# 512-token blocks in the first expert layer of a fused attention and MoE kernel, with attention steps given out once per group

## Chip, core and metric

The kernel runs on one core of one Trainium2 chip. The metric is device time in microseconds (us), the median of several runs; lower is better. Before the change it is 1564.3 us (three runs, 1563.93 to 1564.42).

## What is computed

Cut from the reference, with 8 samples of 576 tokens, 8 heads of 64, pooling by 8:

```python
k_p = k.reshape(B, H, 72, 8, D).mean(axis=3)
v_p = v.reshape(B, H, 72, 8, D).mean(axis=3)
attn = softmax(scale * q @ k_p^T)
x = (attn @ v_p), heads joined             # 4608 x 512
h = max(x @ w1, x @ w2, x @ w3)            # 4608 x 768
x = h @ w_out                              # 4608 x 512
h = x @ w_in ; g = h - tanh(h)             # 4608 x 2048
out = g @ w_out                            # 4608 x 512
```

## The kernel before

Most matrix products are made of three TensorE matmuls on operands that are split into a high and a low part (names ending in H and L). Attention works on tiles of up to 128 query tokens: 40 tiles, five to a sample (four of 128 and one of 64). A tile's steps are `q_split` (L256, L257), `qk` (scores; the first 8 tiles L271 to L273, later ones L279 to L284), `sm_exp` (row maxima on VectorE, eight exponentials on ScalarE, L300, L303), `sm_div` (L311 to L315), `tr_main` and `tr_left` (transposes L331, L342 and their evictions). Tiles are gathered into units; once a unit is complete, four `av` steps (four matmuls each, L352 to L355) write its tokens of x, one step for each group of 128 features, and ScalarE and VectorE evict them (L359, L360). The transposes and `av` share a PSUM tag with two buffers.

The first expert layer, `moe_group` (L513 to L515), works on blocks of `BA` = 384 tokens, 12 blocks. A block has 18 groups (6 feature columns times three weights); a group is 12 matmuls of 128x128 weights on 384 tokens, evicted by ScalarE (first weight, L517) or as a maximum by VectorE (the other two, L519). Four PSUM buffers hold groups. Finished columns go to DRAM (`hs`, L522). The units follow the blocks: 384, 192, 192 and 384 tokens for two samples.

The order of the work is set by the program: `steps` is the list of all attention steps, and `moe_part` hands out parts of it between groups through `attn_to`, so many that `point(x)` is reached by the end; before the change it does so twice in a group, once in its middle (`mid`, after half of its matmuls) and once at its end. The compiler's scheduler moves instructions somewhat from that order, except those under `keep_in_program_order`. The weights come as 64-bit numbers and are converted by `Conv` (one `step` is one 128x512 piece: L88 on ScalarE, L95 to L101 on VectorE, then a split, L122 and L123). The 18 pieces of w1, w2, w3 are converted while attention starts up; the 32 pieces of the second layer's weights while blocks two and later run (`cv.step` in `moe_part`).

Startup: the steps of block 0 run first, with a conversion after each tile's second `sm_exp`; then four groups of block 0 while the attention of block 1 is made, four groups of block 1, and then blocks 0 and 1 by turns (one conversion for every two groups), up to the attention of block 2. From block 2 on each block gives out the attention of later blocks and 4 conversions; it ends in block 9, and blocks 10 and 11 have none. After that come `h @ w_out` (L647 to L649) and the second layer (L705 to L707, L718 to L720), 4104 matmuls of 512 columns, which the change does not touch.

Of the kernel before, what the change touches and what calls it, by code (L numbers as in the profile page):

```python
# [7 lines left out]
F32 = mybir.dt.float32  # L8
# [5 lines left out]
ALU = mybir.AluOpType  # L14
AX = mybir.AxisListType

B, NH, S, D = 8, 8, 576, 64
POOL = 8
SP = S // POOL
NT = B * S  # L20
# [3 lines left out]
NP = NH // 2  # L24
W2 = 2 * SP
KM = 128
KL = W2 - KM
BA = 384
NA = NT // BA
BB = 512  # L30
NB = NT // BB
# [9 lines left out]
TANH_T = 0.6  # L41
QA = (0.28138769604723224, 0.18210311958591932, 0.5012423839837391)
QB = (0.28138769604723224, -0.6558710200885569, 0.1935810566809675)


@with_exitstack
def moe_chain_kernel(ctx, tc, qt, kt, vm, vl, ident, cst, w123, wo1, win, wout, out):
    nc = tc.nc
    V, A, G, T, Q = nc.vector, nc.scalar, nc.gpsimd, nc.tensor, nc.sync
# [84 lines left out]
    at = pool("at", side="right")  # L134
# [16 lines left out]


    units = []
    for b in range(0, B, 2):
        units += [
            (b * S, [(b, 0, 128), (b, 128, 128), (b, 256, 128)]),
            (b * S + 384, [(b, 384, 128), (b, 512, 64)]),
            (b * S + 576, [(b + 1, 0, 128), (b + 1, 128, 64)]),
            (b * S + 768, [(b + 1, 192, 128), (b + 1, 320, 128), (b + 1, 448, 128)]),
        ]  # L160
    tiles = []
    for u, (t0, tl) in enumerate(units):
        off = 0
# [63 lines left out]
    def v_split(b):  # L227
        vs, vx = vsum.pop(b), vxsum.pop(b)
        for i, m in enumerate((m0, m1)):
            A.activation(VH[:, :, 64 * i:64 * i + 64], vs, AF.Copy, scale=m)  # L230
        for i, m in enumerate((e0, e1)):
            A.activation(VX[:, i::2, 64:128], vx, AF.Copy, scale=m[:96])
        for i, m in enumerate((m0, m1)):
            c = slice(64 * i, 64 * i + 64)
            V.scalar_tensor_tensor(out=VL[:, :, c], in0=vs, scalar=m, in1=VH[:, :, c].bitcast(F32),
                                   op0=ALU.mult, op1=ALU.subtract)
        for i, m in enumerate((e0, e1)):
            c = VX[32:64, i::2, 64:128]
            V.scalar_tensor_tensor(out=c, in0=vx[32:64], scalar=m[32:64], in1=c.bitcast(F32),
                                   op0=ALU.mult, op1=ALU.subtract)  # L240

    qraw, qsp, sct, eT = {}, {}, {}, {}

    def q_load(n):
        b, s, cnt = tiles[n][:3]
        t = at.tile([128, NP, 128], F32, tag="qraw", name="qraw", bufs=2)
        Q.dma_start(out=t[:, :, :cnt],
                    in_=qt[b, :, NP * s:NP * (s + cnt)].rearrange("p (c t) -> p c t", c=NP))
        qraw[n] = t

    def q_split(n):
        cnt = tiles[n][2]
        t = qraw.pop(n)[:, :, :cnt]
        h = at.tile([128, NP, 128], F32R, tag="qH", name="qH", bufs=2)
        l = at.tile([128, NP, 128], F32R, tag="qL", name="qL", bufs=2)
        A.copy(h[:, :, :cnt], t)  # L256
        V.tensor_tensor(out=l[:, :, :cnt], in0=t, in1=h[:, :, :cnt].bitcast(F32), op=ALU.subtract)  # L257
        qsp[n] = (h, l)

    scp, nbs = {}, {}  # L260
# [65 lines left out]
    def tr_main(n):  # L326
        b, s, cnt, u, off, _ = tiles[n]
        eH, eL, _ = etile(u)
        ps = ps2.tile([128, NP, 128], F32, tag="tr", name="ps_tr")
        for p in range(NP):  # L330
            T.transpose(ps[:, p, :cnt], sct[n][:cnt, p, :KM], idt[:cnt, :cnt])  # L331
        c = slice(off, off + cnt)
        A.copy(eH[:, :, c], ps[:, :, :cnt])
        V.tensor_tensor(out=eL[:, :, c], in0=ps[:, :, :cnt], in1=eH[:, :, c].bitcast(F32), op=ALU.subtract)

    def tr_left(n):
        b, s, cnt, u, off, _ = tiles[n]
        eX = etile(u)[2]
        lf = lft.pop(n)
        ps = ps2.tile([128, 2, 128], F32, tag="tr", name="ps_tr")  # L340
        for j in range(2):
            T.transpose(ps[:96, j, :cnt], lf[:cnt, j].rearrange("p a b k -> p (a b k)"), idt[:cnt, :cnt])  # L342
        c = slice(off, off + cnt)
        A.copy(eX[:, :, c], ps[:96, :, :cnt])
        V.tensor_tensor(out=eX[64:96, :, c], in0=ps[64:96, :, :cnt], in1=eX[64:96, :, c].bitcast(F32), op=ALU.subtract)

    def av(u, p):
# [11 lines left out]
        A.copy(h, ps[:, :n])  # L359
        V.tensor_tensor(out=l, in0=ps[:, :n], in1=h.bitcast(F32), op=ALU.subtract)  # L360


    steps = []

    def add(fn, *a):
        steps.append((fn, a))

    ntl = len(tiles)
    n_k, n_v = [0], [0]

    def next_k():
        if n_k[0] < B * NP:
            k_load(*divmod(n_k[0], NP))
            n_k[0] += 1
# [23 lines left out]
    def q_step(n):  # L398
        if n < ntl:
            q_split(n)  # L400
        if n + 1 < ntl:
            q_load(n + 1)

    first_tile = {}
    for n, t in enumerate(tiles):
# [3 lines left out]
    for n in range(ntl + 1):  # L409
        last = n == ntl  # L410
        if not last:
            b = tiles[n][0]
            k = n - first_tile[b]
        aux = []
        if not last and b + 1 < B:
            if b == 0:
                if k == 4:
                    aux = [(k_step, 1, p) for p in range(NP)] + [(v_step, 1, i) for i in range(NP + 2)]
            else:
                if k in (2, 3):  # L420
                    aux += [(k_step, b + 1, p) for p in (2 * k - 4, 2 * k - 3)]
                if k in (3, 4):
                    aux += [(v_step, b + 1, i) for i in range(3 * k - 9, 3 * k - 6)]
        if not last:
            add(qk, n, 0)
            add(sm_exp, n, 0)
        if n:
            add(sm_div, n - 1)
        if not last:
            add(qk, n, 1)  # L430
            if aux:
                add(*aux.pop(0))
            add(sm_exp, n, 1)
        if n:
            add(tr_main, n - 1)
            if not last:
                add(q_step, n + 1)
            add(tr_left, n - 1)
        else:
            add(q_step, n + 1)  # L440
        if not last and b and k == 1:
            add(v_split, b)
        avs = [(av, tiles[n - 1][3], p) for p in range(NP)] if n and tiles[n - 1][5] else []
        while avs or aux:
            for l in (avs, aux):
                if l:
                    add(*l.pop(0))
# [12 lines left out]
    def attn_to(i):  # L460
        while pos[0] <= min(i, len(steps) - 1):
            f, a = steps[pos[0]]
            f(*a)
            pos[0] += 1
# [6 lines left out]
    for _ in range(NP - 1):  # L471
        next_k()
    q_load(1)
    Q.dma_start(out=consts, in_=cst)
    cv = Conv(sta, [w123[i] for i in range(18)],
              split_to([tuple(t[i].rearrange("p a b -> p (a b)") for t in (wH, wL)) for i in range(18)], V))
# [14 lines left out]
    for i, (f, a) in enumerate(steps[:block_end[0] + 1]):  # L491
        if f is av and a[1] == 0:
            v_split(0)
        attn_to(i)
        if f is sm_exp and a[1] == 1:
            cv.step()
            for k in (2 * a[0], 2 * a[0] + 1):
                if k < NP + 2:
                    v_step(0, k)
    for _ in range(NP):  # L500
        next_k()

    def moe_group(j, f, m, mid):
        xh, xl = xT[j]
        if m == 0:
            hsb[j, f] = hp.tile([128, BA], F32, tag="h", name="h")
        t = hsb[j, f]
        i = f * 3 + m
        ps = psm.tile([128, 512], F32, tag="mm", name="ps_mm")
        for kc in range(NE):  # L510
            if kc == 2:
                mid()
            T.matmul(ps[:, :BA], wH[i][:, kc], xh[:, kc], start=(kc == 0), stop=False)  # L513
            T.matmul(ps[:, :BA], wH[i][:, kc], xl[:, kc], start=False, stop=False)  # L514
            T.matmul(ps[:, :BA], wL[i][:, kc], xh[:, kc], start=False, stop=(kc == NE - 1))  # L515
        if m == 0:
            A.copy(t, ps[:, :BA])  # L517
        else:
            V.tensor_tensor(out=t, in0=t, in1=ps[:, :BA], op=ALU.max)  # L519
        if m == 2:  # L520
            g, o = divmod(j * BA, HG)
            Q.dma_start(out=hs[g][f][:, o:o + BA], in_=hsb.pop((j, f)))  # L522
# [3 lines left out]
    def moe_part(groups, upto, every=1, conv=lambda k: True):  # L526

        first = pos[0]

        def pace(x):  # L530
            attn_to(first + (upto - first) * x // (2 * len(groups)))

        for k, (j, f, m) in enumerate(groups):
            if every == 1 and conv(k):
                cv.step()
            moe_group(j, f, m, lambda: pace(2 * k + 1))
            if every > 1 and m == 2 and f % 3 < 2:
                cv.step()
            pace(2 * k + 2)

# [3 lines left out]
    def point(x):  # L544

        j = int(x)
        if j >= NA - 1:
# [8 lines left out]
    cv = Conv(sta, srcs, lambda i, w: tc.keep_in_program_order(Q.dma_start(out=wsc[i], in_=w)),  # L556
              tc.keep_in_program_order)
# [173 lines left out]
    for i in range(len(seq) + LAG):  # L731
        if i < len(seq):
            j, c = seq[i]
# [68 lines left out]
```

## Time and profile before

| | |
|---|---|
| median of 3 runs | 1564.3 us |
| time of the profiled execution | 1563.4 us |
| its span, first to last instruction | 1561.5 us |
| PE busy | 1517.3 us, 97% |
| DVE (VectorE) busy | 1165.9 us, 75% |
| ACT (ScalarE) busy | 831.3 us, 53% |
| POOL (GpSimd) busy | 195.4 us, 13% |
| mean granted TensorE clock | 0.995 |

The busy shares are averages over stages with different limits, so the span is read in stages: startup until PE runs without a gap, the blocks with attention between their groups, the last blocks without it, and the two later products. Time outside the span (1.9 us) lies around the program.

### The profile page before, as it was taken

To read this page: it belongs to the slowest core of one execution; us is meant where nothing else is said; L and a number is where in the kernel's file an instruction comes from. 1 tells how busy PE (TensorE), PEld (TensorE's weight loads), DVE (VectorE), ACT (ScalarE), POOL (GpSimd) and SP (SyncE) were. 2 spreads that over 40 slices of the span, in tenths; PEclk is the share of its full clock that TensorE was granted. 3 is DMA by queue.
4 is the path that set the end of the run, shared out by engine and by line. 5 is a ranking of instruction groups with operands and counts; after the bars stand their busy time and mean duration, and the time that the engine had idled before them with its cause. 6 is when DMAs were issued, how large, how long until landed. Compare 5 with 4: busy or idle time off the path is not lost.

```text
span 1561.5 us, 21533 instructions
## 1 busy us (share of the span) xinstructions
PE 1517.3 (97%) x7544; PEld 1337.2 (86%) x7544; DVE 1165.9 (75%) x2086; ACT 831.3 (53%) x2077; POOL 195.4 (13%) x223
## 2 busy tenths in 40 slices
PE   4799999999999999999999999999999999999999
PEld 3699999999999899888888888888888888888887
DVE  8994877777787861443398888888888888888886
ACT  6753655545555630543365555555555555555554
POOL 4510210202010020740001001010101001010000
PEclk9889999999999999999999999999999999999999
DMA  7552445444343330865400001010100000010000
GB/s 239 188 190 64 144 134 167 139 148 154 124 138 102 108 106 31 287 224 164 153 1 27 27 4 52 1 55 1 33 23 27 27 27 28 1 55 1 28 1 27
DMA packets 71213, 134.65 MB, mean 86 GB/s; under 512 B 11840, under 2 KB 21184, under 8 KB 71104
## 3 DMA queue, kind: packets, MB, share of 16 engines
q1 hardware_dynamic: 71104, 133.27, 26.0%
q8 instruction: 59, 0.97, 0.3%
q14 instruction: 50, 0.41, 0.1%
HBM read 91.82 MB, written 41.42 MB: 85 GB/s over the span
## 4 chain that ended last, share of the span: by engine, by line
PE 89%; DVE 6%; ACT 2%; DMA 1%; issue 1%; POOL 0%; SPq 0%; ACTq 0%; DVEq 0%; POOLq 0%
PE ps_mm L513 9%; PE ps_mm L705 8%; PE ps_acc L720 8%; PE ps_mm L706 8%; PE ps_mm L707 8%; PE ps_acc L719 8%; PE ps_acc L718 8%; PE ps_mm L514 8%; PE ps_mm L515 8%; PE ps_acc L648 2%; PE ps_acc L649 2%; PE ps_acc L647 2%; PE ps_mm L648 1%; PE ps_mm L649 1%; PE ps_mm L647 1%; PE ps_sc L279 1%
## 5 line engine op out<-in xcount | busy, mean ns | idle before, releaser
L513 PE MATMUL ps_mm<-xH,wH 128*128 128x384 f32 x864 | 301.4, 349 | 0.0
L514 PE MATMUL ps_mm<-xL,wH 128*128 128x384 f32 x864 | 291.9, 338 | 0.0
L515 PE MATMUL ps_mm<-xH,wL 128*128 128x384 f32 x864 | 291.2, 337 | 0.0
L693 ACT CAST gH<-w 128x512 fp32r<-128x512 f32 x144 | 89.4, 621 | 301.4 <-DVE w L692 301.4
L705 PE MATMUL ps_mm<-ioH,ctH 128*128 128x512 f32 x576 | 224.2, 389 | 0.8 <-ACT ioH L604 0.8
L706 PE MATMUL ps_mm<-ioL,ctH 128*128 128x512 f32 x576 | 224.1, 389 | 0.0
L707 PE MATMUL ps_mm<-ioH,ctL 128*128 128x512 f32 x576 | 224.1, 389 | 0.0
L718 PE MATMUL ps_acc<-ctH,gH 128*128 128x512 f32 x576 | 224.1, 389 | 0.0
L719 PE MATMUL ps_acc<-ctL,gH 128*128 128x512 f32 x576 | 224.1, 389 | 0.0
L720 PE MATMUL ps_acc<-ctH,gL 128*128 128x512 f32 x576 | 224.1, 389 | 0.0
L694 DVE TENSOR_TENSOR gL<-w,gH 128x512 fp32r<-128x512 f32 x144 | 104.1, 723 | 92.1 <-ACT gH L693 87.2
L513 PEld LDWEIGHTS ps_mm<-xH,wH 128*128 128x128 f32 x864 | 163.8, 190 | 1.1 <-DVE h L519 0.2
L514 PEld LDWEIGHTS ps_mm<-xL,wH 128*128 128x128 f32 x864 | 163.8, 190 | 0.0
L515 PEld LDWEIGHTS ps_mm<-xH,wL 128*128 128x128 f32 x864 | 163.1, 189 | 0.0
L519 DVE TENSOR_TENSOR h<-h,ps_mm 128x384 f32<-128x384 f32 x144 | 79.3, 551 | 90.4 <-PE ps_mm L515 82.2
L605 POOL TENSOR_TENSOR ioL<-ioL,ioH 128x512 fp32r<-128x512 f32 x32 | 49.3, 1556 | 728.5 <-ACT ioH L604 728.5
L705 PEld LDWEIGHTS ps_mm<-ioH,ctH 128*128 128x128 f32 x576 | 108.1, 188 | 23.8 <-ACT ioH L604 1.2
L720 PEld LDWEIGHTS ps_acc<-ctH,gL 128*128 128x128 f32 x576 | 108.2, 188 | 22.4
L719 PEld LDWEIGHTS ps_acc<-ctL,gH 128*128 128x128 f32 x576 | 108.1, 188 | 22.5
L706 PEld LDWEIGHTS ps_mm<-ioL,ctH 128*128 128x128 f32 x576 | 108.1, 188 | 22.4
L718 PEld LDWEIGHTS ps_acc<-ctH,gH 128*128 128x128 f32 x576 | 108.1, 188 | 22.4
L707 PEld LDWEIGHTS ps_mm<-ioH,ctL 128*128 128x128 f32 x576 | 108.0, 188 | 22.4
(106 smaller groups left out, 2840.6 us busy)
## 6 DMA issues: line engine op xcount, KB each, us to landing
hs<-h SPq DMA_DIRECT2D x72, 192.0 KB, 1.9
ioL<-hs SPq DMA_DIRECT2D x54, 256.0 KB, 2.9
kraw<-kt SPq DMA_DIRECT2D x32, 288.0 KB, 3.5
raw<-w SPq DMA_DIRECT2D x18, 512.0 KB, 3.7
xs<-ob SPq DMA_DIRECT2D x36, 256.0 KB, 2.1
ioL<-xs SPq DMA_DIRECT2D x36, 256.0 KB, 2.8
out<-ob SPq DMA_DIRECT2D x36, 256.0 KB, 2.2
qraw<-qt SPq DMA_DIRECT2D x32, 256.0 KB, 3.4
```

Source lines behind the costliest of these rows:

```text
L513: T.matmul(ps[:, :BA], wH[i][:, kc], xh[:, kc], start=(kc == 0), stop=False)
L514: T.matmul(ps[:, :BA], wH[i][:, kc], xl[:, kc], start=False, stop=False)
L515: T.matmul(ps[:, :BA], wL[i][:, kc], xh[:, kc], start=False, stop=(kc == NE - 1))
L519: V.tensor_tensor(out=t, in0=t, in1=ps[:, :BA], op=ALU.max)
L693: A.copy(gH, w)
L694: V.tensor_tensor(out=gL, in0=w, in1=gH.bitcast(F32), op=ALU.subtract)
L705: T.matmul(ps, wh[:, kc], xh, start=(kc == 0), stop=False)
L706: T.matmul(ps, wh[:, kc], xl2, start=False, stop=False)
L707: T.matmul(ps, wl_[:, kc], xh, start=False, stop=(kc == NE - 1))
L718: T.matmul(acc, gH[:, r], oh, start=(c == 0), stop=False)
L719: T.matmul(acc, gH[:, r], ol, start=False, stop=False)
L720: T.matmul(acc, gL[:, r], oh, start=False, stop=(c == NC2 - 1))
```

## The change

`BA` becomes 512: 9 blocks, and a group's 12 matmuls take 512 tokens. Units are now the pieces into which the block borders cut each sample (`pieces`): 512+64, 448+128, 384+192, 320+256 and the same mirrored, 16 units and 40 tiles as before. Three raw query tiles are buffered and loaded two ahead. The transposes of a tile become one step `tr`. In the startup the conversions come after all attention steps of block 0 rather than between them, and the K loads of the next sample before its last tile. In `moe_part`, groups of block 2 and later give out no attention in their middle, and six conversions a block rather than four. The query split of the tiles in block 2 (the third) is pinned to program order.

```diff
-BA = 384
+BA = 512
+def pieces(b):
+
+    at = [0] + [x - b * S for x in range(0, NT, BA) if b * S < x < b * S + S] + [S]
+    return list(zip(at, at[1:]))
...
-    for b in range(0, B, 2):
-        units += [
-            (b * S, [(b, 0, 128), (b, 128, 128), (b, 256, 128)]),
-            (b * S + 384, [(b, 384, 128), (b, 512, 64)]),
-            (b * S + 576, [(b + 1, 0, 128), (b + 1, 128, 64)]),
-            (b * S + 768, [(b + 1, 192, 128), (b + 1, 320, 128), (b + 1, 448, 128)]),
-        ]
+    for b in range(B):
+        for i, (s, e) in enumerate(pieces(b)):
+            units.append((b * S + s, [(b, t, min(128, e - t)) for t in range(s, e, 128)]))
...
-        t = at.tile([128, NP, 128], F32, tag="qraw", name="qraw", bufs=2)
+        t = at.tile([128, NP, 128], F32, tag="qraw", name="qraw", bufs=3)
...
-        V.tensor_tensor(out=l[:, :, :cnt], in0=t, in1=h[:, :, :cnt].bitcast(F32), op=ALU.subtract)
+        r = V.tensor_tensor(out=l[:, :, :cnt], in0=t, in1=h[:, :, :cnt].bitcast(F32), op=ALU.subtract)
+        if units[tiles[n][3]][0] // BA == 2:
+            tc.keep_in_program_order(r)
...
-            add(tr_main, n - 1)
+            add(tr, n - 1)
             if not last:
                 add(q_step, n + 1)
-            add(tr_left, n - 1)
...
+        if f is qk and a == (3, 0):
+            for _ in range(NP):
+                next_k()
         attn_to(i)
         if f is sm_exp and a[1] == 1:
-            cv.step()
...
-    for _ in range(NP):
-        next_k()
+    for _ in range(4):
+        cv.step()
...
-            moe_group(j, f, m, lambda: pace(2 * k + 1))
-            if every > 1 and m == 2 and f % 3 < 2:
+            moe_group(j, f, m, (lambda: pace(2 * k + 1)) if j < 2 else lambda: None)
+            if every > 1 and m == 2:
                 cv.step()
```

How the instructions move, at three places. First VectorE at the start, after the row maxima of the first tile (`nb`). Before:

```order
L300 TENSOR_REDUCE nb<-ps_sc 128x4 x2
L95 TENSOR_SCALAR ma<-ma 128x512
L97 TENSOR_SCALAR ma<-ma 128x512
L99 SCALAR_TENSOR_TENSOR ma<-raw,ma 128x512
L101 SCALAR_TENSOR_TENSOR ma<-raw,ma 128x512
L311 TENSOR_SCALAR su<-su 128x8
L312 RECIPROCAL su<-su 128x8
L313 TENSOR_TENSOR sc<-sc,su 128x576
```

and with the change (L101, L103 and L105 are now the conversion's lines, L259 the query split, L315 to L317 the division):

```order
L304 TENSOR_REDUCE nb<-ps_sc 128x4 x2
L259 TENSOR_TENSOR qL<-qraw,qH 128x512
L315 TENSOR_SCALAR su<-su 128x8
L316 RECIPROCAL su<-su 128x8
L317 TENSOR_TENSOR sc<-sc,su 128x576
L304 TENSOR_REDUCE nb<-ps_sc 128x4
L101 TENSOR_SCALAR ma<-ma 128x512 x2
```

The four conversion instructions that stood between the first tile's maxima and its division are gone from there. Counted over VectorE's list up to the last piece of x of block 1, there are 2 conversions fewer, 2 tiles more and one half of a sample's K sums more than before.

Second, PE where a tile of a later block is transposed (`sc` main part, `lf` leftover). Before:

```order
L515 MATMUL ps_mm<-xH,wL_154 128x384
L331 MATMUL ps_tr<-idt,sc 128x128 x4
L513 MATMUL ps_mm<-xH,wH_137 128x384
L514 MATMUL ps_mm<-xL,wH_137 128x384
L515 MATMUL ps_mm<-xH,wL_155 128x384
L513 MATMUL ps_mm<-xH,wH_137 128x384
L514 MATMUL ps_mm<-xL,wH_137 128x384
L515 MATMUL ps_mm<-xH,wL_155 128x384
L342 MATMUL ps_tr<-idt,lf 96x128 x2
```

and with the change, in the last block that has attention:

```order
L525 MATMUL ps_mm<-xH,wL_166 128x512
L335 MATMUL ps_tr<-idt,sc 128x128 x4
L346 MATMUL ps_tr<-idt,lf 96x128 x2
L523 MATMUL ps_mm<-xH,wH_148 128x512
L524 MATMUL ps_mm<-xL,wH_148 128x512
```

The main and leftover transposes now follow each other directly, and more expert matmuls stand in one piece. Over the whole list PE goes from expert matmuls to attention matmuls 125 times, 189 times before.

Third, PE between the second and the third `av` of a unit, which share PSUM buffers with the first. Before, in block 3:

```order
L355 MATMUL ps_av<-eL,VH 128x192
L513 MATMUL ps_mm<-xH,wH_134 128x384
L514 MATMUL ps_mm<-xL,wH_134 128x384
L515 MATMUL ps_mm<-xH,wL_152 128x384
L513 MATMUL ps_mm<-xH,wH_134 128x384
L514 MATMUL ps_mm<-xL,wH_134 128x384
L515 MATMUL ps_mm<-xH,wL_152 128x384
L352 MATMUL ps_av<-eH,VH 128x192
```

and with the change, in block 5, at a unit of 128 tokens:

```order
L359 MATMUL ps_av<-eL,VH 128x128
L523 MATMUL ps_mm<-xH,wH_143 128x512
L356 MATMUL ps_av<-eH,VH 128x128
L357 MATMUL ps_av<-eH,VL 128x128
L358 MATMUL ps_av<-eX,VX 128x128
L359 MATMUL ps_av<-eL,VH 128x128
L524 MATMUL ps_mm<-xL,wH_143 128x512
```

Six expert matmuls stood there, and now one; at most other places there are twelve now.

## Rows read from the trace of the kernel before

**Rows 1.** The page: span, and busy time, share and instructions of each engine.
```profile
span 1561.5 us, 21533 instructions
PE 1517.3 (97%) x7544; PEld 1337.2 (86%) x7544; DVE 1165.9 (75%) x2086; ACT 831.3 (53%) x2077; POOL 195.4 (13%) x223
```
**Rows 2.** Busy time of each engine by stretches of the span, with clock and DMA.
```profile
core 0: us, PE busy (x) PEld busy (x) DVE busy (x) ACT busy (x) POOL busy (x), PEclk, DMA share, GB/s
0.00:8.00 8.00, 0.46 (x1) 0.29 (x1) 2.33 (x5) 2.83 (x6) 3.64 (x9) 1.00 0.77 241
8.00:83.60 75.60, 50.03 (x238) 42.57 (x238) 71.35 (x147) 52.47 (x210) 38.73 (x60) 0.91 0.63 209
83.60:160.00 76.40, 76.40 (x443) 76.16 (x443) 52.99 (x114) 34.22 (x107) 0.33 (x1) 0.98 0.37 118
160.00:560.00 400.00, 393.59 (x2382) 382.33 (x2381) 304.98 (x693) 231.18 (x869) 52.37 (x87) 1.00 0.43 139
560.00:626.10 66.10, 66.10 (x382) 65.88 (x381) 22.60 (x36) 8.88 (x18) 4.66 (x3) 1.00 0.12 42
```
**Rows 3.** PE's timeline (start, us, engine, line): expert matmuls, 384 and 512 columns.
```profile
599.76 0.33 PE L514 MATMUL ps_mm<-xL,wH 128*128 128x384 f32 x1
...
625.76 0.33 PE L514 MATMUL ps_mm<-xL,wH 128*128 128x384 f32 x1
...
1199.12 0.39 PE L718 MATMUL ps_acc<-ctH,gH 128*128 128x512 f32 x1
...
1203.88 0.39 PE L718 MATMUL ps_acc<-ctH,gH 128*128 128x512 f32 x1
```
**Rows 4.** PE's timeline: two neighbours of an `av` of 192 tokens.
```profile
524.37 0.28 PE L354 MATMUL ps_av<-eX,VX 96*128 96x192 f32 x1
524.48 0.27 PE L355 MATMUL ps_av<-eL,VH 128*128 128x192 f32 x1
```
**Rows 5.** PE's timeline: going over from expert matmuls to attention and back.
```profile
226.77 0.29 PE L279 MATMUL ps_sc<-kbd,qH 128*64 128x288 f32 x1
...
227.17 0.39 PE L513 MATMUL ps_mm<-xH,wH 128*128 128x384 f32 x1
227.39 0.34 PE L514 MATMUL ps_mm<-xL,wH 128*128 128x384 f32 x1
...
228.28 0.60 PE L331 MATMUL ps_tr<-idt,sc 128*128 128x128 f32 x4
228.64 0.42 PE L513 MATMUL ps_mm<-xH,wH 128*128 128x384 f32 x1
228.90 0.33 PE L514 MATMUL ps_mm<-xL,wH 128*128 128x384 f32 x1
```
**Rows 6.** VectorE busy (x) on tiles `ma`, `sc`, `ps_tr`, `qL`, `xL`, `ksum`, in this order.
```profile
0.00:626.10 626.10, 144.50 (x242) 0.99 0.42 136
0.00:626.10 626.10, 94.35 (x232) 0.99 0.42 136
0.00:626.10 626.10, 40.86 (x80) 0.99 0.42 136
0.00:626.10 626.10, 27.03 (x40) 0.99 0.42 136
0.00:626.10 626.10, 29.03 (x64) 0.99 0.42 136
0.00:626.10 626.10, 32.64 (x54) 0.99 0.42 136
```
**Rows 7.** PE's waits from 160 to 560 us: us in total, times, longest.
```profile
PE ps_av L352 <- DVE xL L360: 2.6, 5, 0.8
PE ps_sc L279 <- DVE sc L284: 1.2, 2, 0.9
```
**Rows 8.** ScalarE's timeline: first and last exponential of the first tile.
```profile
12.93 0.32 ACT L303 ACTIVATE sc<-ps_sc,nb 128x72 f32<-128x72 f32 x1 [0.99 <-DVE nb L300]
...
15.02 0.35 ACT L303 ACTIVATE sc<-ps_sc,nb 128x72 f32<-128x72 f32 x1
```

More of the change, by code (lines that the diff above doesn't have):

```diff
@@ L360, in av, with tr @@
         V.tensor_tensor(out=l, in0=ps[:, :n], in1=h.bitcast(F32), op=ALU.subtract)
+    def tr(n):
+        tr_main(n)
+        tr_left(n)
     steps = []
@@ L400, in q_step @@
             q_split(n)
-        if n + 1 < ntl:
-            q_load(n + 1)
+        if n + 2 < ntl:
+            q_load(n + 2)
     first_tile = {}
@@ L473, in moe_chain_kernel @@
     q_load(1)
+    q_load(2)
     Q.dma_start(out=consts, in_=cst)
@@ L769 @@
     qp = q.reshape(B, NP, 128 // D, S, D).transpose(0, 2, 4, 1, 3).reshape(B, 128, NP, S)
-    cuts = {0: (0, 128, 256, 384, 512, 576), 1: (0, 128, 192, 320, 448, 576)}
+    cuts = [[t for s, e in pieces(b) for t in range(s, e, 128)] + [S] for b in range(B)]
     qt = np.stack([
-        np.concatenate([qp[b, :, :, s:e].reshape(128, NP * (e - s)) for s, e in zip(cuts[b % 2], cuts[b % 2][1:])], axis=1)
+        np.concatenate([qp[b, :, :, s:e].reshape(128, NP * (e - s)) for s, e in zip(cuts[b], cuts[b][1:])], axis=1)
         for b in range(B)
```

## Prediction, made before the result was known

> **What bounds the kernel.** The page comes first: PE is busy for 97% of the span [rows 1], so the time is PE's work plus the 44.2 us in which PE stands still. The second view, the busy time by stretches, says where. From the start to 83.6 us PE is idle for 7.5 and 25.6 us; from 83.6 to 160 us it has no gap; from 160 to 560 us it loses 6.4 us; up to 626.1 us nothing [rows 2]. What is left, 4.7 us, lies behind 626.1 us, which the change does not touch. In the stretch from 8 to 83.6 us VectorE is busy for 71.35 of 75.6 us [rows 2]: it makes x for blocks 0 and 1 and converts weights, so VectorE bounds the start. After that PE does. A change of block size therefore has three places to act: the price of PE's work, the VectorE work ahead of the moment from which PE runs without a gap (for short, the filling point), and the waits afterwards.
>
> The third view, PE's timeline, gives the price of an expert matmul. Between the two rows of 384 columns lie 150 matmuls and 26.00 us, between the two of 512 columns 21 and 4.76 us [rows 3]: 173.3 and 226.7 ns. The reader is to see that the pitch, not the 0.33 or 0.39 us of a row, is the cost, since matmuls overlap. At the granted clock of 1.00 [rows 2], that is the 2.4 GHz level, 384 and 512 columns take 160.0 and 213.3 ns; 13 ns are left over in each, whatever its width.
>
> **The change, part by part.** The sum is made against the profiled execution, 1563.4 us (span 1561.5 and 1.9 around it); the median of the runs is 0.9 higher.
>
> *Fewer, wider expert matmuls.* 12 x 18 x 12 = 2592 at 173.3 ns are 449.2 us; 9 x 18 x 12 = 1944 at 226.7 ns are 440.7 us: **-8.5 us**, all of it on PE. The evictions get fewer and wider and the bytes to DRAM stay the same; with VectorE at 76% and the DMA share at 0.43 between 160 and 560 us [rows 2] both stay beside PE's work. Were that cover gone, the eviction would be late for one of four PSUM buffers, which is the first rival.
>
> Against this speaks a rule of the Trainium skill ("TensorE: Matmul & The Clock Gate", Back-to-back issue gap): a warm matmul takes its columns at 2.4 GHz and only 2.5 ns more. By it the term would be 2592 x 162.5 - 1944 x 215.8 ns, or -1.7 us; the rows have 13 ns and decide.
>
> *The `av` matmuls.* There are 256 before and after. Before, 128 have 384 columns and 128 have 192, the latter at 0.11 us [rows 4]: 22.2 + 14.1 = 36.3 us. After, 32 each have 512, 448, 384, 320 and 256 columns, at columns / 2.4 GHz + 13 ns 0.227, 0.200, 0.173, 0.147 and 0.120 us, and 96 have 192, 128 or 64. The trace shows no `av` below 192 columns. The price is at most the 0.11 us of the nearest row, and at least what the line gives (0.04 and 0.07 us for 64 and 128). I take 0.11, because the 192-column row already lies above its line (0.093): 27.7 + 10.6 = 38.3 us, **+2.0 us**, with the other end at -1.5 us.
>
> *Fewer changes of work on PE.* Behind four score matmuls the next expert matmul takes 0.22 us to its successor, behind transposes 0.26 us [rows 5], where 0.173 is normal: 0.05 and 0.09 us for each return. The order has 64 returns fewer. 27 of them are those between a tile's main and leftover transposes: 27 x 0.09 + 37 x 0.05 = **-4.3 us**. The ends are 0 (if 512 columns make the return dearer, which no row excludes) and 64 x 0.09 = -5.8 us.
>
> *The start.* Up to the last x of block 1, VectorE's list has two tiles more. A tile costs it (94.35 + 40.86 + 27.03 + 29.03) / 40 = 4.8 us [rows 6], so +9.6 us; half a sample's K sums, 32.64 / 16 = +2.0 us; and two conversions fewer at 5 x 144.50 / 242 = 3.0 us [rows 6], -6.0 us. That is +5.6; the row sums, reciprocals and wider evictions that these rows leave out make it about +7 us, by which the filling point moves. But PE has done more when it gets there: 51 matmuls of 512 for 48 of 384 (+3.2), four more sets of scores at 0.40 us (+1.6) and two tiles' transposes at 0.36 us for the main part [rows 5] and about 0.1 for the rest (+0.9), and `av` of 512, 448 and 64 for 384, 192 and 192 (+2.3): +8.0 us. So the idle time changes by **-1 us**. The clock averages 0.91 there [rows 2] and should again. The ends: -5 us, if the 4.2 us that VectorE still lost after 8 us go too, and +10 us by the first rival. The queue of loads is no bound: two raw weight pieces fewer are due, against two query tiles, and the DMA share is 0.63 [rows 2]. The postponed conversions are the next to be late: between the filling point and the 18th there are about 12 x 3.0 us of them, ten maxima and three tiles on VectorE, some 55 us with the maxima at 0.5 us or a little more each, against 14 groups of 2.72 and three tiles on PE. A tile there costs PE (542.5 - 2544 x 0.1733 - 6.4) / 32 = 3.0 us [rows 2, 3], so 47 us. The lag of 8 us is just what three groups in PSUM allow.
>
> *The waits afterwards.* A third `av` waits for the first to be evicted: five waits, 2.6 us [rows 7], where one `av` (0.44 us) and six expert matmuls (1.04 us) stood between. So 2.0 us are needed. With the change two places have only an `av` between, one an `av` and one expert matmul (0.67 us): 1.55 + 1.55 + 1.35 = 4.4 us. Two have an `av` of 320 or 384 tokens and three expert matmuls (about 1.3 us): together 1.4 us. Score buffers, which cost 1.2 us [rows 7], have three expert matmuls between at two places rather than six: about 2 us. The rest, 6.4 - 2.6 - 1.2 = 2.6 us, I keep. That is 10.4 for 6.4, **+4 us**. The ends are -4 us (elsewhere twelve matmuls, 2.72 us, now stand between steps) and +12 us, the second rival. Giving out steps once per group is this term; it issues nothing new. The pinned splits and the third query buffer add no instruction.
>
> *The sum:* -8.5 + 2.0 - 4.3 - 1 + 4 = -7.8 us, so 1555.6 us for a profiled execution and 1556.5 us as a median.
>
> **The rivals.**
> 1. *VectorE runs dry in the start, and the kernel is slower.* The conversions filled VectorE while ScalarE made a tile's exponentials, which take 2.4 us (12.93 to 15.37) [rows 8]. In the new list only two of four come before the first x. If all four tiles of block 0 wait that long, the filling point comes 4 x 2.4 = 9.8 us later; and the lag of 8 us then passes the cover in PSUM for some 4 us more. 1556.5 + 13.8 = 1570 us. For it: VectorE has little else there. Against it: two conversions and the query splits remain, tile follows tile with two buffers each, and VectorE's need to convert only falls. It decides from about 8 us of extra VectorE waits before the first expert matmul.
> 2. *Denser attention eats the gain.* 26 tiles now lie in five blocks, 30 in eight before: 9.4 us of expert work a tile rather than 10.0, and six conversions a block. If each short distance drags the next step along, the waits grow by 12 instead of 4 us: 1564.5 us. For it: VectorE's share was 76% already. Against it: from 160 to 560 us PE lost only 1.6%.
> 3. *The gain is larger.* The wider spacing takes waits away (-3 instead of +4) and the start loses VectorE's gaps (-4 instead of -1): 1546.5 us.
> 4. *The 13 ns are not a matmul's own.* If they grew with the columns, the first term would be nothing: 1565 us. Both pitches [rows 3] speak against it. The skill's 2.5 ns would come to nearly this.
>
> **How the numbers follow.** Forecast 0.47, with its own range 1551 to 1562 us; rival 1 0.13, rival 2 0.20, rival 3 0.17, rival 4 0.03. A measurement of this kernel can tell about 0.2%, 3.1 us, from no change, so faster is below 1561.2 and slower above 1567.4. Faster: 0.40 of the forecast, all of rival 3 and 0.03 of rival 2, 0.60. Same: 0.07 + 0.14 + 0.03 of rival 4, 0.24. Slower: rival 1 and 0.03 of rival 2, 0.16. The range 1545 to 1567 us leaves out rival 1 and the last third of rival 3, 0.19 together.
>
> **What the changed profile would show.** Expert matmuls 0.227 us apart; fewer busy us of LDWEIGHTS; PE without gaps from about 90 us on, with some 33 us idle before; about 10 us of waits up to the last attention step, most at the third `av`; the end of the first layer about 8 us sooner than 626.1. Wrong would be a pitch of 512 columns above 0.23 us among attention work, VectorE with more than 12 us idle between 8 us and the filling point, or PE idle in blocks 2 to 6 by more than 15 us.

## The result and the profile after

The change takes 1551.03 us in the median of three runs (1550.85 to 1551.72) against 1564.3 us: a ratio of 0.9917, 95% interval 0.9904 to 0.9931. The forecast was 1556.5 us, so the direction held and the gain came out larger, 13.3 instead of 7.8 us. The time lies at the lower edge of the forecast's own range, 1551 to 1562 us. The profiled execution took 1550.85 us, its span 1548.8 us.

The page's first lines of the change, beside [rows 1]:

```profile
span 1548.8 us, 20108 instructions
PE 1508.3 (97%) x6896; PEld 1250.4 (81%) x6896; DVE 1154.0 (75%) x2050; ACT 823.5 (53%) x2059; POOL 195.5 (13%) x223
```

Weight loads are busy for 87 us less (648 matmuls fewer), PE for 9 us less. Where the gain lies is seen in the busy time by stretches of the change, to be held against [rows 2]:

```profile
core 0: us, PE busy (x) PEld busy (x) DVE busy (x) ACT busy (x) POOL busy (x), PEclk, DMA share, GB/s
0.00:8.00 8.00, 0.46 (x1) 0.29 (x1) 2.50 (x5) 2.99 (x7) 3.65 (x9) 1.00 0.75 245
8.00:83.60 75.60, 53.66 (x244) 44.48 (x244) 71.01 (x153) 57.38 (x235) 35.50 (x60) 0.90 0.68 214
83.60:160.00 76.40, 76.16 (x353) 63.46 (x354) 62.84 (x131) 40.80 (x137) 12.43 (x18) 0.96 0.47 148
160.00:560.00 400.00, 393.88 (x1962) 327.89 (x1961) 297.73 (x654) 217.63 (x805) 48.35 (x72) 1.00 0.42 135
```

Up to 83.6 us PE is busy for 3.6 us more; from 160 to 560 us it loses 6.1 us where it lost 6.4. The first layer ends at 613.5 instead of 626.1 us, 12.6 us sooner, and what follows is as long as before. PE's timeline of the change gives its returns to expert matmuls, behind transposes (at 229.72 us) and behind scores (at 302.73 us), and the new pitch (104 matmuls lie between the last two rows):

```profile
229.58 0.38 PE L346 MATMUL ps_tr<-idt,lf 128*96 128x128 f32 x2
229.72 0.47 PE L524 MATMUL ps_mm<-xL,wH 128*128 128x512 f32 x1
230.03 0.39 PE L525 MATMUL ps_mm<-xH,wL 128*128 128x512 f32 x1
...
302.66 0.23 PE L285 MATMUL ps_sc<-kbd,qL 128*128 128x144 f32 x1
302.73 0.44 PE L523 MATMUL ps_mm<-xH,wH 128*128 128x512 f32 x1
303.01 0.40 PE L524 MATMUL ps_mm<-xL,wH 128*128 128x512 f32 x1
...
589.66 0.39 PE L523 MATMUL ps_mm<-xH,wH 128*128 128x512 f32 x1
...
613.23 0.39 PE L525 MATMUL ps_mm<-xH,wL 128*128 128x512 f32 x1
```

That is 23.57 us / 104 = 226.6 ns, as in [rows 3], and a return costs 0.28 - 0.227 = 0.05 us behind scores and 0.31 - 0.227 = 0.08 us behind transposes, 0.05 and 0.09 us with 384 columns [rows 5]. PE's waits from 160 to 560 us, beside [rows 7], and the three of them that fall on the third `av`:

```profile
PE ps_av L356 <- DVE xL L364: 3.3, 3, 1.7
PE ps_tr L335 <- DVE sc L317: 1.5, 1, 1.5
PE ps_av L356 <- DVE eL L338: 0.6, 1, 0.6
PE ps_sc L283 <- DVE sc L288: 0.6, 1, 0.6
```
```profile
212.84 0.36 PE L356 MATMUL ps_av<-eH,VH 128*128 128x192 f32 x1 [1.69 <-DVE xL L364]
...
364.50 0.36 PE L356 MATMUL ps_av<-eH,VH 128*128 128x192 f32 x1 [0.92 <-DVE xL L364]
...
425.14 0.33 PE L356 MATMUL ps_av<-eH,VH 128*128 128x128 f32 x1 [0.65 <-DVE xL L364]
```

These are the three places named beforehand; no other third `av` waits for an eviction, and scores wait once, for 0.6 us.

**A balance.** Up to the start of the second layer, time is PE's idle time, the time lost at the lower clock, and the rest, which is PE's work at full clock. I add the loss over stretches of 4 us as busy time times (1 - granted clock); that overstates it where little of PE's work slows, so the last column is good to some 4 us. The rows are of the profiled execution of each kernel, in us, which can lie off the median: e1's took 1561.4 us, the fastest of its eleven and 4 us under their median; e3's, e5's, e8's and e9's lie 2 to 3 us off. Run names are explained below.

```
kernel                      median  2nd layer  idle   idle     lower  work
                                    from       0-160  160-560  clock
before                      1564.3  626.1      33.1   6.4       6.8   579.8
the change                  1551.0  613.5      29.7   6.1       7.7   569.9
e1 conversions between      1565.4  623.9      36.9   6.3      10.7   570.0
e2 steps given out twice    1553.8  615.4      30.3   8.1       6.9   570.1
e3 transposes in two steps  1558.8  623.6      33.1   5.9      16.4   568.2
e4 384 columns, all else    1564.2  626.1      29.7   6.8      15.7   573.9
e5 512 columns alone        1563.9  623.8      39.7   4.9       6.0   573.2
e6 384, conversions behind  1559.7  622.2      28.2   6.9      10.4   576.7
e7 no pin                   1551.8  615.2      28.6   6.1      10.6   569.9
e8 low parts on GpSimd      1560.8  621.9      35.1   5.6      14.2   567.0
e9 three pieces first       1561.9  626.2      36.7   6.5      15.6   567.4
e10 five pieces first       1557.3  619.7      32.2   6.0      15.7   565.8
e11 512, conversions behind 1557.4  618.8      31.4   4.9      12.7   569.8
e12 three, own queue        1557.5  621.5      31.9   8.1      11.0   570.5
```

So the change does 9.9 us less work (-10.8 was forecast for the first three terms), stands still for 3.7 us less, and loses 1.0 us more at the lower clock.

### The profile page after: what moved, and what is told of

Its sections match the earlier page's. It is cut to its first block, busy times and chain, and to the rows that moved or that the text cites. A ratio compares the mean times of both kernels' runs of the same rounds, so it can differ in the third digit from the quotient of the medians.

```text
span 1548.8 us, 20108 instructions
## 1 busy us (share of the span) xinstructions
PE 1508.3 (97%) x6896; PEld 1250.4 (81%) x6896; DVE 1154.0 (75%) x2050; ACT 823.5 (53%) x2059; POOL 195.5 (13%) x223
## 4 chain that ended last, share of the span: by engine, by line
PE 89%; DVE 8%; ACT 1%; issue 1%; DMA 0%; ACTq 0%; DVEq 0%; SPq 0%
PE ps_mm L715 8%; PE ps_mm L717 8%; PE ps_acc L730 8%; PE ps_acc L728 8%; PE ps_acc L729 8%; PE ps_mm L716 8%; PE ps_mm L523 8%; PE ps_mm L524 8%; PE ps_mm L525 8%; PE ps_acc L659 2%; PE ps_acc L658 2%; PE ps_acc L657 2%; PE ps_mm L659 1%; PE ps_mm L658 1%; PE ps_mm L657 1%; PE ps_sc L283 1%
## 5 line engine op out<-in xcount | busy, mean ns | idle before, releaser
L523 PE MATMUL ps_mm<-xH,wH 128*128 128x512 f32 x648 | 260.0, 402 | 0.0
L524 PE MATMUL ps_mm<-xL,wH 128*128 128x512 f32 x648 | 254.2, 392 | 0.0
L525 PE MATMUL ps_mm<-xH,wL 128*128 128x512 f32 x648 | 253.8, 392 | 0.0
L529 DVE TENSOR_TENSOR h<-h,ps_mm 128x512 f32<-128x512 f32 x108 | 73.9, 685 | 104.2 <-PE ps_mm L525 102.9
L525 PEld LDWEIGHTS ps_mm<-xH,wL 128*128 128x128 f32 x648 | 121.9, 188 | 25.9
L523 PEld LDWEIGHTS ps_mm<-xH,wH 128*128 128x128 f32 x648 | 122.6, 189 | 22.7
L524 PEld LDWEIGHTS ps_mm<-xL,wH 128*128 128x128 f32 x648 | 122.4, 189 | 22.5 <-DVE xL L364 0.3
```

## Experiments

The first four ran together (the kernel before had 1563.85 us there), then e5 to e8 (1564.42), e9 to e11 (1564.23) and e12 (1563.78). Each ratio is to the kernel before of its own group. The change's three runs had their own (1564.3); a difference from the change is one of medians.

**e1: conversions between the first tiles again.**

```diff
         if f is sm_exp and a[1] == 1:
+            if a[0] < 4:
+                cv.step()
             ...
-    for _ in range(4):
-        cv.step()
```

> The changed kernel, but the first four conversions stand between the tiles of block 0 again. Theory S (the start got shorter because conversions no longer sit ahead of the attention in VectorE's list): PE's idle time before it fills grows by 3 to 4 us, the time is 1554 to 1555 us. Theory F (the start got shorter because PE holds more work when it fills: wider matmuls, two more tiles done): the time stays within 1 us of the changed kernel, 1550 to 1552 us.

1565.36 us, ratio 1.0006 (0.9997 to 1.0014): the whole gain is gone, far more than the 3 to 4 us of the larger expectation, though the work is the same 570 us. Two things are lost in its trace, whose execution is 10.5 us slower than the change's; the other 4 us of the median are in no trace. First, PE is idle for 4.4 us more up to 100 us, and the last x of block 1 comes 4.0 us later (below, e9). Second, PE stands still again at 137 us, long after it had run without gaps, and then runs at the lower clock. PE's timeline of e1, and its windows around:

```profile
139.65 0.33 PE L285 MATMUL ps_sc<-kbd,qL 128*128 128x144 f32 x1 [2.87 <-DVE qL L259]
```
```profile
136.00:140.00 4.00, 1.13 (x7) 0.73 (x6) 3.97 (x8) 1.04 (x3) 2.00 (x2) 1.00 0.41 131
140.00:144.00 4.00, 4.00 (x13) 3.14 (x13) 3.87 (x8) 1.33 (x4) 0.00 (x0) 0.57 0.52 142
```

**e2: steps given out twice per group in all blocks.**

```diff
-            moe_group(j, f, m, (lambda: pace(2 * k + 1)) if j < 2 else lambda: None)
+            moe_group(j, f, m, lambda: pace(2 * k + 1))
```

> The changed kernel, but groups of all blocks give out attention steps in their middle as well. By its order there are 25 more returns of PE from attention to expert matmuls, and none of the five short distances between the avs of one unit. Theory G (giving out once saves returns): 25 x 0.05 to 0.09 = +1.3 to +2.3 us against waits of 3.3 us less, 1549 to 1551 us. Rival (once or twice changes nothing that PE waits for): 1550.5 to 1551.5 us with the waits still there.

1553.81 us, ratio 0.9933 (0.9921 to 0.9945): 2.8 us of the gain, though this interval overlaps the change's (0.9904 to 0.9931), and slower than both expectations. The waits of a third `av` shrink from 3.3 to 0.7 us, but waits for scores (3.6 us) and for the transposed low parts (3.1 us) take their place, 8.1 instead of 6.1 us in all.

**e3: the two transposes apart again.**

```diff
-            add(tr, n - 1)
+            add(tr_main, n - 1)
             if not last:
                 add(q_step, n + 1)
+            add(tr_left, n - 1)
```

> The changed kernel, but a tile's main and leftover transposes are apart again, with the query split between them. 19 more returns of PE and two more short distances between avs. If a return costs 0.05 to 0.09 us: +1 to +1.7 us, and up to 2 us of waits: 1552 to 1555 us. If a return costs nothing: 1551 to 1552 us.

1558.76 us, ratio 0.9965 (0.9953 to 0.9976), 7.7 us slower than the change and slower than both expectations. By the balance the work is no larger, although it has 19 returns more; the loss is 3.4 us of idle time in the first 160 us and about 9 us at the lower clock.

**e4: everything but the width.**

```diff
-BA = 512
+BA = 384
-            if every > 1 and m == 2:
+            if every > 1 and m == 2 and f % 3 < 2:
```

> The changed kernel with blocks of 384 tokens (12 blocks, units of 384 and 192, four conversions a block), every other edit kept. Theory W (the width is worth 8.5 us on the expert matmuls, less 2 us on the avs): 1551 + 6.5 = 1557.5 us, PE's pitch 0.173 us. If the start's gain also needs the width (theory F above): 1560 to 1562 us. If the gain came from the order of the rest and not from the width: below 1555 us.

1564.21 us, ratio 0.9999 (0.9991 to 1.0008), outside all three expectations. The other edits alone give no time: the work falls by 6 us and idle time by 3 us, and the lower clock takes 9 us more. Block 0 is three tiles here, so the conversions behind it come earlier, and PE has no expert matmul for a while. The window from 60 to 80 us of e4, first all of PE's work, then that on the `ps_mm` tiles alone:

```profile
60.00:80.00 20.00, 14.15 (x58) 11.42 (x58) 19.36 (x44) 14.77 (x61) 9.46 (x13) 0.50 0.52 164
```
```profile
60.00:80.00 20.00, 0.00 (x0) 0.00 (x0) 0.00 (x0) 0.00 (x0) 0.50 0.52 164
```

None of the 58 matmuls is an expert's (15 are in the kernel before, 25 in the change), and the clock is at its lower level, 1.2 GHz, for all of the stretch; in the same window it is 0.84 and 0.81 there.

**e5: the width alone.** The edits of e1, e2, e3 and e7 together, and two query buffers. The earlier K loads stay, here and in e11.

> The change's wide blocks with nearly all the rest undone: conversions between the first tiles, two splits for the two tables of transposes, steps given out twice a group, no pin, two query buffers. Theory B (a balance: up to the second layer PE needs 570 us of work at full clock with 512 columns and 580 with 384, and what differs beside that is PE's idle time and the time lost at the lower clock): work 572 to 575 us (47 returns more than the change), idle 40 to 46, clock 7 to 14, so a second layer that begins at 621 to 633 us and 1557 to 1571 us in all, near 1565, as without the width. Theory W (the width is a gain in itself): 1553 to 1558. Theory A (the losses of undoing the edits one by one add up, 14 + 3 + 8 us): 1573 to 1579.

1563.85 us, ratio 0.9998 (0.9989 to 1.0006), near the 1565 that the balance gave: work 573, idle 44.6, clock 6.0 us. The width saves its work and the start gives it back. Theory W falls, and so does the sum of single losses: those of e1, e2 and e3 are partly the same loss.

**e6: the kernel before, conversions behind block 0's attention.**

```diff
         if f is sm_exp and a[1] == 1:
-            cv.step()
             ...
+    for _ in range(4):
+        cv.step()
```

> The kernel before, with four conversions behind block 0's attention instead of one behind each of its tiles. If the place of the conversions is a gain in itself (theory S, the 10 us that the change lost without it): 1551 to 1558. If it needs 512 columns, because with 384 block 0 is three tiles and PE then runs out of expert matmuls while VectorE converts (theory F): 1561 to 1568, with idle time up to 100 us within 3 us of before.

1559.65 us, ratio 0.9970 (0.9959 to 0.9982): between the two expectations. The place of the conversions is worth 4.8 us by itself with 384 columns (4.4 us less idle time, 3.6 us more at the lower clock, 3.1 us less work in the balance, which is within its error).

**e7: no pin.** The pin of the query splits in block three taken out.

> The change without the pinned query splits of block three. The pin only sets VectorE's order in one block. Theory P0 (nothing): 1549 to 1553, with the second layer from 612.5 to 615 us. Theory P (the pin holds a query split back from being taken early or late, so that scores wait): 1553 to 1557, with more idle time of PE between 200 and 300 us.

1551.75 us, ratio 0.9918 (0.9905 to 0.9932): the pin is worth nothing that can be measured.

**e8: low parts of the weights on GpSimd.**

```diff
-              split_to([... for i in range(18)], V))
+              split_to([... for i in range(18)], G))
```

> The change with the low halves of the first 18 weight pieces (18 subtractions of 0.706 us on VectorE) made on GpSimd, where such a subtraction takes 1.8 us. Theory V (VectorE's list sets the start): eight of them lie before PE runs without a gap, 5.6 us; PE is idle for 2 to 5 us less up to 100 us and the kernel takes 1545 to 1549. Theory X (a GpSimd operation behind reductions that wait for loads comes late, or both engines slow each other on SBUF): expert matmuls wait for a wL, 1552 to 1560.

1560.84 us, ratio 0.9976 (0.9967 to 0.9986), 10 us slower than the change: the time of theory X, but not its waits, since no expert matmul waits for a wL. A subtraction took 1.26 to 1.60 us on GpSimd. Nine low parts are now done before block 1's x, which comes at 97.8 us, instead of six and 92.5: VectorE had run the rest of those conversions ahead of it. And some of VectorE's other instructions got longer. The same group on VectorE between 8 and 96 us, the change first, then e8:

```profile
L315 DVE TENSOR_SCALAR su<-su 128x8 f32<-128x8 f32 x8 | 2.1, 258 | 1.7 <-ACT sc L307 1.7
```
```profile
L315 DVE TENSOR_SCALAR su<-su 128x8 f32<-128x8 f32 x8 | 3.4, 422 | 1.7 <-ACT sc L307 1.6
```

**e9 and e10: three or five weight pieces first.** The change makes four pieces behind block 0's attention and then runs four groups of each of blocks 0 and 1 before it interleaves them. For three:

```diff
-    for _ in range(4):
+    for _ in range(3):
         cv.step()
...
-    moe_part(gr(0)[:4], point(2), conv=lambda k: k == 0)
-    moe_part(gr(1)[:4], point(2.2))
-    moe_part([g for p in zip(gr(0)[4:], gr(1)[4:]) for g in p], ...)
+    moe_part(gr(0)[:3], point(2), conv=lambda k: k == 0)
+    moe_part(gr(1)[:3], point(2.2))
+    moe_part([g for p in zip(gr(0)[3:], gr(1)[3:]) for g in p], ...)
```

> The change with three weight pieces and three groups of blocks 0 and 1 ahead of the interleaved rest, instead of four. One conversion (3.0 us of VectorE, 3.4 us as slowed in the start) goes from before block 1's x to behind it, and one group of block 0 (2.7 us at full clock, up to 5.4 us at the lower) goes from the stretch at the lower clock to the stretch at full clock. Theory V (VectorE's list up to block 1's x sets the start, and the clock makes early PE work dear): block 1's x 3 us sooner, 1547 to 1550. Theory C (what PE can do meanwhile counts just as much): 1550 to 1553. Theory X (the scheduler puts other VectorE work ahead, or conversions come late afterwards and scores wait at 130 to 140 us, as in the run with the conversions between the tiles): 1555 to 1562.

> The opposite: five weight pieces and five groups ahead. Theory V: block 1's x 3 us later, 1553 to 1556. Theory C: 1550 to 1553. Theory X (any other order of VectorE's list than the change's runs into waits): 1555 to 1562.

1561.86 us (0.9982, 0.9970 to 0.9994) and 1557.32 us (0.9957, 0.9945 to 0.9969): both slower than the change, theory X. e9's ten executions are spread over 9 us (1556.7 to 1565.8); the traced one took 1563.75 us. The first half of theory V is seen in VectorE's timelines: the last x of block 1 comes at 87.7 us in e9 with 5 pieces ahead of it, at 91.2, 92.5 and 93.1 in e2, the change and e7 with 6, at 95.4 in e11 with 7, at 95.9, 96.4, 96.5 and 97.6 in e3, e10, e1 and e5 with 8. Two pieces more than the change has come with 3.4 to 5.1 us. The count is not all: e12 below has 5 and 91.6 us.

What e9 then loses lies at 125 to 135 us. PE's and the other engines' waits there, from 120 to 140 us of e9:

```profile
ACT ma L94 <- DMA raw<-w: 10.8, 3, 9.1
...
PE ps_sc L285 <- DVE qL L259: 8.1, 1, 8.1
DVE ma L101 <- ACT ma L94: 7.6, 1, 7.6
```

PE's scores wait for a query split, which stands on VectorE behind a conversion, which waits for ScalarE, which waits for a raw weight piece. SP's timeline of e9 shows why that is late: its queue issues in order, and the piece (L88) stands behind loads of values (L211), which wait for buffers that GpSimd's sums free. Issued at 123.3 us, it is used at 130.0. First SP's waits from 110 to 130 us, then its timeline:

```profile
SPq L211 <- POOL vsum L207: 4.2, 2, 2.4
SPq L211 <- POOL vxsum L207: 3.9, 2, 2.2
```
```profile
117.68 5.06 SPq L211 DMA_DIRECT2D vraw<-vm  x3
122.83 0.38 SPq L532 DMA_DIRECT2D hs<-h  x1
123.31 0.89 SPq L88 DMA_DIRECT2D raw<-w  x2
```

**e11: width and conversions behind, all other edits undone.**

> Wide blocks and the conversions behind block 0's attention, all other edits undone (two splits of the transposes, steps given out twice a group, no pin, two query buffers). Theory I (width and place of the conversions are one edit in effect; the rest is worth a little): 1553 to 1557. Theory A (the rest is worth the 8 and 3 us that undoing it cost one by one): 1560 to 1564.

1557.39 us, ratio 0.9954 (0.9942 to 0.9966): just above theory I, 6.8 us less than the kernel before, where the width alone gave nothing and the conversions alone 4.8 us. The other edits undone here are worth the remaining 6.4 us: less than the sum of what e2 and e3 lost.

**e12: e9 with the values' loads of samples 2 to 7 in GpSimd's queue.**

```diff
-        Q.dma_start(out=t, in_=vm[b, p]...)
+        (G if b > 1 else Q).dma_start(out=t, in_=vm[b, p]...)
```

The two loads of `vl` are edited the same way. VectorE, PE and ScalarE keep their order.

> The run with three pieces first, and the loads of values of samples 2 to 7 issued from GpSimd's queue instead of SP's; VectorE, PE and ScalarE keep their instructions in the same order. In the run with three pieces first PE stood for 8.1 us at 126 to 135 us behind a query split, VectorE behind ScalarE, ScalarE 9.1 us for a raw weight piece whose load SP had issued only after the loads of values, which wait for buffers that GpSimd frees. Theory Q (that queue is the cause): the 8.1 us go to under 2, with them some 2 us at the lower clock, so about 10 us: 1550 to 1554 instead of 1561.9. Theory V (the piece is late because its transfer is, or VectorE's list is too long): PE still waits 5 us or more there, 1557 to 1563.

1557.48 us, ratio 0.9964 (0.9955 to 0.9974). The same waits as shown for e9, now in e12 from 120 to 146 us:

```profile
ACT ma L94 <- DMA raw<-w: 2.9, 3, 2.3
...
PE ps_sc L285 <- DVE qL L259: 1.0, 1, 1.0
```

So the queue was the cause of that wait: 8.1 us became 1.0, with nothing moved on the three engines. The load no longer stands behind those of values, and from its issue to its use it takes 4.6 us (121.0 to 125.6) where it took 6.7. The time fell by 4.4 us only, not by 10 (2.8 us, if each run is held against the kernel before of its group): block 1's x now comes at 91.6 instead of 87.7 us, although VectorE's list is the same. VectorE's instructions up to there take 3.4 us longer in all. Row by row the two lists part where single ones stretch, here the same two of e9 and then of e12:

```profile
65.75 0.42 DVE L101 TENSOR_SCALAR ma<-ma 128x512 f32<-128x512 f32 x1
...
68.74 0.74 DVE L317 TENSOR_TENSOR sc<-sc,su 128x576 f32<-128x576 f32 x1
```
```profile
67.47 2.07 DVE L101 TENSOR_SCALAR ma<-ma 128x512 f32<-128x512 f32 x1
...
72.15 1.43 DVE L317 TENSOR_TENSOR sc<-sc,su 128x576 f32<-128x576 f32 x1
```

GpSimd was busy for 13.2 us between 60 and 80 us in e12, for 10.6 in e9; 3.3 us of e12's are the loads that it now issues. Its timeline of e12 has sums beside both stretched rows:

```profile
67.82 1.42 POOL L205 TENSOR_TENSOR vxraw<-vxraw 96x256 f32<-96x256 f32 x2
...
72.22 0.74 POOL L205 TENSOR_TENSOR vraw<-vraw 128x256 f32<-128x256 f32 x1
```

In e9 sums ran beside the same two instructions as well (L207 at 65.72, L206 at 68.91 us), and they did not stretch. So what stretched them is not shown; nor is it shown that the same kernel run again would keep the 91.6 us. None of the twelve beat the change.

## Why the prediction held, and where it was off

*Fewer, wider matmuls, `av`, and returns:* -8.5, +2.0 and -4.3 us, -10.8 together; the balance shows -9.9, within its error. The pitch of 226.6 ns and the returns of 0.05 and 0.08 us are measured on the new kernel as taken from the old one. By the 2.5 ns of the Trainium skill ("TensorE: Matmul & The Clock Gate", Back-to-back issue gap), which the section gives for a matmul by itself and not for a stream in which each has its weight load, the pitch would be 215.8 ns; the rows here, of such a stream, decide for 13 ns over the columns. An `av` of 64 tokens, which no row had shown, came at 0.11 us, the upper end that was taken:

```profile
59.03 0.28 PE L358 MATMUL ps_av<-eX,VX 96*128 96x64 f32 x1
59.14 0.28 PE L359 MATMUL ps_av<-eL,VH 128*128 128x64 f32 x1
```

*The start:* -1 us was forecast. Idle time up to 160 us fell by 3.4 us, and 1.0 us went to the clock, so -2.4. VectorE's list was sized rightly: +7 us forecast for the last x of block 1, and it moved from 85.6 to 92.5 us. The step that failed is "by which the filling point moves": PE does not wait for the end of that list. The prediction took 83.6 us for the filling point, where a run of expert matmuls begins; PE's last gap ended before that, at 81.70 us, and with the change at 84.86 us. PE's rows there and VectorE's last x of block 1, first before, then with the change:

```profile
81.70 0.53 PE L352 MATMUL ps_av<-eH,VH 128*128 128x192 f32 x1 [1.80 <-DVE xL L360]
85.61 0.34 DVE L360 TENSOR_TENSOR xL<-ps_av,xH 128x192 fp32r<-128x192 f32 x1
```
```profile
84.86 0.74 PE L356 MATMUL ps_av<-eH,VH 128*128 128x448 f32 x1
92.48 0.62 DVE L364 TENSOR_TENSOR xL<-ps_av,xH 128x448 fp32r<-128x448 f32 x1
```

Both gaps end with an `av` of block 1's last unit. Before, the two moments lay 3.9 us apart; after, PE's own work (`av` of 448 columns, scores, expert matmuls) covers 7.6 us of VectorE's list. So the moment moved by 3.2 instead of 7 us, and PE had been busy for 6.7 instead of 8.0 us more by then: both terms were too large, and because their errors cancel in part, their difference came out at -3.5 instead of -1 us.

*The waits afterwards:* +4 us was forecast, -0.3 came; this is the mis-sized term that makes most of the difference between 7.8 and 12.6 us. The three shortest distances cost 3.3 instead of 4.4 us (1.69, 0.92 and 0.65 for 1.55, 1.55 and 1.35). The 1.4 us for an `av` of 320 or 384 tokens and most of the 2 us for score buffers did not come (0.6 did), and of the 2.6 us that were kept 2.1 are there. In the last stretch of attention, 520 to 560 us, PE loses nothing now and lost 3.0 us before. So 10.4 us were forecast and 6.1 came. That giving out once is part of this is seen in the waits: e2 has 8.1 us of them without it.

*Two sentences that were too easy.* "The queue of loads is no bound" was argued from a DMA share of 0.63. In the change it is true: from 110 to 145 us ScalarE waits 4.4 us for raw pieces and PE for nothing above 0.13 us. In e9 the queue's order held a weight piece and cost 8.1 us while the share was no bound either. And "add no instruction" was enough for the pin (e7); e1 and e3 add next to no work either, only move it, and cost 14 and 8 us.

*The rivals.* Rival 1 (VectorE dry while ScalarE makes exponentials) did not come: VectorE is busy for 71.01 of 75.6 us, as before [rows 2]. Its price has the size of the other order's loss only by chance: with the conversions between the tiles, which it held to be the safer place, the kernel is 14 us slower (e1), while VectorE is idle there for 6.5 of the 75.6 us, only 1.9 more than in the change. Rival 2 (waits grow by 12 us) fell with the waits term. Rival 3 (larger gain, waits -3 and start -4) describes what came best in direction, at 2.7 of its 7 us. Rival 4 fell with the pitch. That the forecast's direction and range held owes something to luck: the start came near by two errors that cancel in part, and the waits term was wrong by 4.3 us.

*What the study shows and leaves open.* Shown: the other edits without the width bring no time (e4), nor does the width alone (e5), whose work saved is given back by idle time. The conversions' place is the edit on which most hangs: put back, it takes the whole gain (e1); with the width alone, it brings 6.8 of the 13.3 us (e11). Shown too, for e9: a queue that holds a load back can cost PE 8 us (e12). Less clear is whose the saved work is: the balance has 6.6 us less with the width alone (e5) and 5.9 us less with all but the width (e4), together more than the change's 9.9, within its error of some 4 us each. That the number of pieces ahead of block 1's x sets that moment is only argued, since e12 with 5 has it as late as e2 with 6. Only argued as well: that merging the transposes helps by VectorE's order in the start; e3 differs there in PE's idle time and in the clock, and I cannot tell which came first. The third query buffer was undone only together with other edits, and the earlier K loads and the six conversions a block in no run with 512 tokens.

## What to carry to other kernels

A saving of work on the bound engine reaches the time only if the start still fills that engine, so cost an edit of tile size together with the order of the feeding engine's list up to the first gapless moment, and take that moment from the bound engine's own work, not from the feeder's last item. A balance of idle time, time at the lower clock and work, over the same stretch of each run, shows where kernels of one width differ: here their work agrees within some 7 us (565.8 to 573.2), while idle time and the clock differ by up to 10 us each. Look at the in-order queue of loads for what stands behind a load that waits for a buffer: its busy share says nothing about that.

## What the runs showed of the hardware

**The clock after a short wait.** A wait of 1.69 us at the third `av` left the granted clock at 1.00 in the change (up to 212.84 us), and a wait of the same length was followed by the lower level in e3 (up to 219.08 us). Windows around it, the change first, then e3:

```profile
208.00:212.00 4.00, 3.15 (x20) 2.58 (x18) 3.02 (x8) 3.26 (x13) 0.00 (x0) 1.00 0.05 16
212.00:216.00 4.00, 3.16 (x16) 2.71 (x17) 3.40 (x9) 1.41 (x4) 0.46 (x2) 1.00 0.69 216
216.00:220.00 4.00, 3.99 (x22) 3.15 (x21) 1.45 (x5) 2.95 (x14) 0.53 (x3) 1.00 0.65 197
```
```profile
216.00:220.00 4.00, 2.08 (x13) 1.74 (x12) 3.62 (x9) 1.62 (x6) 0.00 (x0) 0.84 0.23 82
220.00:224.00 4.00, 4.00 (x14) 3.32 (x14) 2.60 (x8) 3.41 (x13) 0.64 (x3) 0.50 0.63 184
224.00:228.00 4.00, 4.00 (x18) 3.34 (x17) 0.76 (x3) 1.84 (x7) 1.38 (x4) 0.80 0.51 164
```

In e3 the lower level then costs 0.3 + 2.0 + 0.8 = 3.1 us (busy time times what the clock lacks), more than the wait itself; in the change the same wait cost nothing beyond its length. In e3 PE had also stood still for 0.23 us just before (up to 216.69 us); whether that decides, or something else, was not tried.

**VectorE beside GpSimd.** In e12 single VectorE instructions took 2 to 5 times as long as in e9 (0.42 to 2.07 us, 0.74 to 1.43) with the same list. The Trainium skill ("SBUF — State Buffer", Who interferes with whom) has VectorE and GpSimd share a pair of ports: where a VectorE instruction uses its two-port mode, whichever of the two engines issues first holds the pair for its whole instruction and the other blocks; a VectorE instruction with two inputs in SBUF contends with GpSimd's reads. These rows agree in kind, but the sums beside the unstretched rows of e9 show that running side by side does not settle it, and the cause stays open. Work moved from VectorE to GpSimd need not shorten the start: e8 took 0.7 us for each low part off VectorE's list, and the last x of block 1 came 5.3 us later.
